# Attention loads on ScalarE's queue, a re-spaced order of attention groups and a wider spacing of Sinkhorn steps, ahead of a two-layer expert network

## The chip, the cores and the metric

One core of one Trainium2 chip. The metric is the device time of one execution in microseconds (us), lower is better. Engines: TensorE (PE; PEld is its weight load), VectorE (DVE), ScalarE (ACT), GpSimd (POOL) and SyncE (SP), which issues the DMAs.

## What is computed

Three stages, all in fp32. Attention over q, k, v of shape (4 batches, 8 heads, 576, 64), where the first four heads see a local band and the last four a stride:

```python
rel = pos[:, None] - pos[None, :]
mask_local = (rel >= 0) & (rel < 32)
mask_strided = (rel >= 0) & (pos[None, :] % 32 == pos[:, None] % 32)
attn = softmax(where(mask, q @ k.T / 8, -1e9));  x = attn @ v      # -> (2304, 512)
```

Then a mixture of eight experts with a dense gate, balanced by eight Sinkhorn steps:

```python
P = exp(x @ w_gate - max)
for _ in range(8):
    P /= P.sum(1, keepdims=True) + 1e-9
    P /= P.sum(0, keepdims=True) + 1e-9
    P *= N / E                                   # 2304 / 8
out = sum(P[:, e:e+1] * (relu(x @ w1[e]) @ w2[e]) for e in range(8))
```

and last a feed-forward layer, `h = out @ w_in; (h * sigmoid(1.702 * h)) @ w_out`, with 2048 hidden columns.

## The kernel before

The expert and feed-forward part is cut into units. A unit is one slice of 256 hidden columns for one block of 768 tokens; the first 32 units (4 per expert) belong to the first block. Each fp32 matrix is split into a high and a low part in fp32r, and each product is six matmuls. A unit of the first block is a list of 13 *pieces*: seven products that combine quarters of the input and of the weights (line 1038), and six pieces of the way back (`tile_down`, lines 1304 to 1306). Weights of the first block are loaded raw, split on ScalarE (high part, line 270 or 280) and GpSimd or DVE (low part, line 264), and stored split to DRAM from SyncE's queue (line 268) for the later blocks. `advance` issues the next piece and the side tasks that are due with it; side tasks are kept in a table by piece number. The program order of each engine's instructions is fixed by the order in which they are written; every engine works its own list in order, and so does SyncE with its DMAs.

Attention comes first and is software-pipelined over `groups` (line 876). A group (b, pair, g) with g of 0 to 2 is a third of the positions of one pair of local heads; (b, pair, -1), called compact, is a whole pair of strided heads, gathered by class. In step i, `att_step` writes scores for group i, the exponentials for group i - 1, normalisation for i - 2, the transpose for i - 3 and the products with v for i - 4, so 32 groups take 36 steps. A compact group's transpose (line 715, on DVE) is copied by four small copies into a block-diagonal operand, `wide` (lines 717 to 723), of which there is one. Its products with v (line 739) are evacuated on DVE (line 872). After the products of a compact group a filler comes before the next transpose, from step 10 on.

Between the parts of a step stand calls of a filler. In steps 0 to 9 it issues dummy matmuls (`keep_warm`, line 1451), IDLE_GAP of them per call; in steps 10 to 15 pieces at a rate of 0.6 per call and dummies otherwise; from step 16 on 1.5 pieces per call, three calls per step. Pieces 33, 35 and 37 hold no matmul.

The q/k tiles and the v tiles of attention have two buffers each (two early pairs have tiles of their own). `LOAD_QK` and `LOAD_V` give the step in which a pair's load is written: as early as the buffer's last reader is written, and not more than two steps ahead of the scores (three ahead of the products with v). The loads are issued by SyncE at the end of the step (lines 641, 648).

After the attention comes the gate: `gate_steps` is a list of small tasks, one for each piece from piece 106 on. A Sinkhorn iteration is `sinkhorn_rows` (five DVE operations, lines 985 to 992), three empty places, and `sinkhorn_cols` (one matmul, line 996, and four DVE operations, lines 998 to 1001), so five pieces. `last_rows` transposes the result on TensorE (line 1010). The experts' first twelve units don't use the gate yet.

Of the kernel before, what the change touches and what calls it, by code (L numbers as in the profile page):

```python
# [12 lines left out]
ALU = mybir.AluOpType  # L13
# [18 lines left out]
IDLE_FIRST = 6  # L32
IDLE_GAP = 1.0

# [23 lines left out]
def strided_attention_moe_ffn(  # L58
# [573 lines left out]

    def load_qk(b, pair, c=slice(0, S)):
        if (b, pair) in EARLY:
            if not spare:
                spare.append(tok.tile([P, 2, 2, S], F32, tag="tok", name="qkt"))
            t = spare[0][:, pair]
            nc.sync.dma_start(out=t[:, :, c], in_=qk[b, pair][:, :, c])
        else:
            t = ap.tile([P, 2, S], F32, tag="qk", name="qkt")  # L640
            nc.sync.dma_start(out=t, in_=qk[b, pair])
        att_in["qk", b, pair] = t

    def load_v(b, pair):
        t = ap.tile([P, CQ, P], F32, tag="v", name="vt")
        compact = pair >= NPAIR // 2
        src = vc[b, pair - NPAIR // 2] if compact else vw[b, pair]
        nc.sync.dma_start(out=t if compact else t[:, : vw.shape[3]], in_=src)
        att_in["v", b, pair] = t
# [62 lines left out]
    def compact_transpose(i, b, pair):  # L712
# [4 lines left out]
        for c in range(CG):  # L717
            rows = slice(c * Q, c * Q + CLEN)
            o = wide[rows, :, c * CLEN : (c + 1) * CLEN]
            if c % 2:  # L720
                nc.gpsimd.tensor_copy(o, src[rows, :, :CLEN])
            else:
                nc.scalar.activation(out=o, in_=src[rows, :, :CLEN], func=AF.Copy)
# [151 lines left out]

    groups = [(0, 0, 0), (0, 1, 0), (0, 0, 1), (0, 1, 1), (0, 2, -1), (0, 3, -1)]
    NHALF = len(groups)
    groups += [(0, 0, 2), (0, 1, 2), (1, 2, -1), (1, 3, -1), (1, 0, 0), (1, 1, 0)]
    NFIRST = len(groups)
    groups += [(1, 0, 1), (1, 0, 2), (1, 1, 1), (1, 1, 2)]  # L880
    for b in range(2, B):
        groups += [(b, pair, -1) for pair in PAIRS[:2]]
        groups += [(b, pair, g) for pair in PAIRS[2:] for g in range(3)]
    NALONE = NHALF + 1
# [8 lines left out]

    pairs = [(b, pair) for b in range(B) for pair in PAIRS]
    at = {p: [i for i, x in enumerate(groups) if x[:2] == p] for p in pairs}
# [10 lines left out]
    def att_step(i, fill):  # L906
# [3 lines left out]
        def run(d, stage):  # L910
# [5 lines left out]
            return stage(i - d, b, pair, g) or ()  # L916

        if i < NHALF + 4:
            for d, stage, gap in STAGES:
# [4 lines left out]
        else:  # L924
# [12 lines left out]
            for t in third[:1]:  # L937
                t()
            run(1, att_exp)
            fill()  # L940
            for t in third[1:]:
                t()
            fill()
        for p in LOAD_QK[i]:
            load_qk(*p)
        for p in LOAD_V[i]:
            load_v(*p)

# [45 lines left out]
    def sinkhorn_cols():  # L994
# [4 lines left out]
        nc.vector.reciprocal(out=cr, in_=cr)  # L999
        nc.vector.tensor_scalar_mul(cr, cr, float(NT) / E)  # L1000
        nc.vector.tensor_tensor(
            out=pr, in0=pr, in1=cr[:, None, :].to_broadcast([P, NTT, E]), op=ALU.mult
        )
# [11 lines left out]
    def gate_steps():  # L1015
        steps = [lambda blk=blk: gate_logits(blk) for blk in range(1, NB)] + [gate_max]
        steps += [lambda: None, gate_max_row, lambda: None, gate_max_all, lambda: None, gate_exp]
        for _ in range(SINKHORN):
            steps += [sinkhorn_rows, lambda: None, lambda: None, lambda: None, sinkhorn_cols]
        steps += [lambda: None, last_rows]  # L1020
        return steps
# [421 lines left out]
    with tc.manual_schedule():  # L1443
# [56 lines left out]

        ahead[NHALF + 1].append(lambda: split_input(0))
        ahead[NHALF + 3].append(lambda: split_input(3))
# [146 lines left out]
```

## Time and profile before

| | |
|---|---|
| median of 3 runs | 1975.1 us (1974.87 to 1975.49) |
| the profiled execution, its own time | 1973.61 us |
| its span, first to last instruction | 1971.8 us |
| PE busy, share of the span | 1920.8 us, 97% |
| DVE busy | 1456.3 us, 74% |
| POOL busy | 1248.0 us, 63% |
| ACT busy | 847.9 us, 43% |
| mean granted TensorE clock | 0.988 of 2.4 GHz |
| DMA | 546.19 MB, mean 277 GB/s |

Read it so: TensorE is the engine that is nearly always busy, and the chain of work that ended last runs through it for 74% of the span. What it lacks to full use lies early: the page's slices show it at 8 to 9 tenths in the first sixth of the span and at 9 or more from there on. Busy shares of a whole span hide this, so the rows below are taken by stage.

### The profile page before, as it was taken

How to read it: one execution, taken by the hardware profiler on the slowest of the kernel's cores; microseconds unless marked ns; L12 is line 12 of the kernel's file. 1: busy time of each engine (PE TensorE's matmuls, PEld its weight loads, DVE VectorE, ACT ScalarE, POOL GpSimd, SP SyncE). 2: the span in 40 equal slices, each digit the busy share in tenths (PEclk: the TensorE clock that was granted, in tenths of full speed). 3: DMA queues.
4: the chain of work that ended last, by engine and by line, in shares of the span. 5: the costliest groups of instructions: out<-in, count | busy, mean ns of one | idle time of the engine just before them, and what ended most of it. 6: DMA issues, size and time to landing. Idle time of an engine off the chain costs nothing.

```text
span 1971.8 us, 35140 instructions
## 1 busy us (share of the span) xinstructions
PE 1920.8 (97%) x11701; PEld 1794.1 (91%) x11701; DVE 1456.3 (74%) x2723; ACT 847.9 (43%) x2071; POOL 1248.0 (63%) x1290
## 2 busy tenths in 40 slices
PE   8988998999999999999999999999999999999999
PEld 6777787888888999999999999999999998888888
DVE  5776677676777788787877788888887766756555
ACT  4554455666766333333333433333333335533332
POOL 3555565786778677777677887888887767700100
PEclk7999999999999999999999999999999999999999
DMA  6557687999998888898998789999989867765653
GB/s 237 172 195 254 222 294 254 370 346 354 357 338 292 300 305 293 288 289 276 301 298 288 249 294 310 338 332 314 355 307 324 297 204 269 250 195 182 223 193 122
DMA packets 284452, 546.19 MB, mean 277 GB/s; under 512 B 30864, under 2 KB 52720, under 8 KB 283376
## 3 DMA queue, kind: packets, MB, share of 16 engines
q1 hardware_dynamic: 283984, 543.61, 80.4%
q8 instruction: 94, 1.54, 0.3%
q14 instruction: 86, 0.70, 0.1%
q10 hardware_dynamic: 288, 0.34, 0.1%
HBM read 382.30 MB, written 161.53 MB: 276 GB/s over the span
## 4 chain that ended last, share of the span: by engine, by line
PE 74%; DVE 3%; DMA 2%; POOL 1%; issue 1%; ACT 0%; SPq 0%; DVEq 0%; ACTq 0%; POOLq 0%
PE y L1199 22%; PE pA L1038 20%; PE pC L1038 10%; PE y L1306 6%; PE y L1305 6%; PE y L1304 5%; PE pB L1038 5%; DMA s1moe<-w 1%; DMA acc<-kept 0%; POOL s L1171 0%; DVE xs L565 0%; DMA w<-s7moe 0%; POOL comb L1146 0%; DMA s7moe<-w 0%; DVE r L1152 0%
## 5 line engine op out<-in xcount | busy, mean ns | idle before, releaser
L1038 PE MATMUL pA<-xc,w 128*128 128x384 f32 x2880 | 573.0, 336 | 2.2 <-DVE pB L1094 2.1
L1199 PE MATMUL y<-comb,w 128*128 128x384 f32 x2688 | 537.5, 334 | 2.5 <-DMA w<-s7moe 1.5
L1038 PEld LDWEIGHTS pA<-xc,w 128*128 128x128 f32 x2880 | 508.6, 188 | 19.4 <-DVE pB L1094 4.0
L1199 PEld LDWEIGHTS y<-comb,w 128*128 128x128 f32 x2688 | 472.1, 188 | 3.6 <-DVE r L1152 1.8
L1146 POOL TENSOR_TENSOR comb<-s,comb 128x384 fp32r<-128x384 f32 x256 | 283.5, 1118 | 87.2 <-ACT comb L1141 81.4
L1209 DVE TENSOR_TENSOR sum<-y,sum 128x384 f32<-128x384 f32 x420 | 231.0, 551 | 100.2 <-PE y L1199 98.0
L1038 PE MATMUL pC<-xc,w 128*128 128x384 f32 x1464 | 295.8, 336 | 0.0
L1306 PE MATMUL y<-w,hl 128*128 128x512 f32 x672 | 269.2, 401 | 5.8 <-DVE hl L1078 5.6
L1304 PE MATMUL y<-w,hh 128*128 128x512 f32 x672 | 265.4, 395 | 7.6 <-DVE x L863 3.5
L1038 PEld LDWEIGHTS pC<-xc,w 128*128 128x128 f32 x1464 | 259.7, 188 | 9.8
L1305 PE MATMUL y<-w,hh 128*128 128x512 f32 x672 | 267.0, 397 | 0.0
L1141 ACT ACTIVATE comb<-r 128x384 fp32r<-128x384 f32 x192 | 101.0, 526 | 365.8 <-DVE r L1152 354.8
L1306 PEld LDWEIGHTS y<-w,hl 128*128 128x128 f32 x672 | 126.9, 189 | 36.5 <-DVE hl L1078 9.0
L1304 PEld LDWEIGHTS y<-w,hh 128*128 128x128 f32 x672 | 127.1, 189 | 28.0 <-DVE x L863 4.1
L1038 PE MATMUL pB<-xc,w 128*128 128x384 f32 x708 | 142.1, 335 | 0.0
L270 ACT ACTIVATE w<-raw 128x256 fp32r<-128x256 f32 (+1 forms) x307 | 135.6, 460 | 14.2 <-POOL raw L234 11.5
L1305 PEld LDWEIGHTS y<-w,hh 128*128 128x128 f32 x672 | 127.0, 189 | 15.9
L1146 POOL TENSOR_TENSOR comb<-r,comb 128x384 fp32r<-128x384 f32 x64 | 67.6, 1056 | 116.2 <-ACT comb L1141 116.1
L264 POOL TENSOR_TENSOR w<-raw,w 128x512 fp32r<-128x512 f32 (+1 forms) x104 | 121.3, 1182 | 30.2 <-ACT w L270 30.0
L1141 ACT ACTIVATE comb<-s 128x384 fp32r<-128x384 f32 x256 | 131.5, 514 | 11.9 <-POOL s L1171 11.8
L1171 POOL TENSOR_TENSOR s<-r,r 128x384 f32<-128x384 f32 x127 | 135.1, 1084 | 2.1 <-DVE r L1152 2.0
L1333 DVE TENSOR_TENSOR acc<-y,acc 128x512 f32<-128x512 f32 x126 | 86.8, 689 | 63.7 <-PE y L1306 63.6
(179 smaller groups left out, 2824.0 us busy)
## 6 DMA issues: line engine op xcount, KB each, us to landing
w<-s1moe SPq DMA_DIRECT2D x448, 256.0 KB, 4.9
w<-s7moe SPq DMA_DIRECT2D x448, 256.0 KB, 4.9
s1moe<-w SPq DMA_DIRECT2D x216, 256.0 KB, 4.9
w<-s1ffn SPq DMA_DIRECT2D x133, 256.0 KB, 2.7
s7moe<-kw SPq DMA_DIRECT2D x116, 256.0 KB, 4.7
s7moe<-w SPq DMA_DIRECT2D x96, 256.0 KB, 4.8
w<-s2ffn SPq DMA_DIRECT2D x38, 512.0 KB, 3.7
raw<-wa SPq DMA_DIRECT2D x32, 512.0 KB, 6.0
```

The lines of the kernel that those rows point to most:

```text
L264: eng.tensor_tensor(out=t[:, 1], in0=src, in1=f(high), op=ALU.subtract)
L270: nc.scalar.activation(out=high, in_=src, func=AF.Copy)
L1038: nc.tensor.matmul(out=o, lhsT=w[:, hw, kk * P : (kk + 1) * P], rhs=x[:, hx, kk, :], start=opens and m == 0, stop=ends and m == len(todo) - 1,
L1141: nc.scalar.activation(out=t[:, 0, :], in_=part[i, q], func=AF.Copy)
L1146: eng.tensor_tensor(out=t[:, 1, :], in0=part[i, q], in1=f(t[:, 0, :]), op=ALU.subtract)
L1171: eng.tensor_tensor(out=part[i, q], in0=part[i, a], in1=part[i, b], op=op)
L1199: nc.tensor.matmul(out=o, lhsT=t[:, hw, dt * P : (dt + 1) * P], rhs=x[:, hx, :], start=(n == 0), stop=(n == 5))
L1209: nc.vector.tensor_tensor(out=a, in0=o, in1=a, op=ALU.add)
L1304: nc.tensor.matmul(out=o, lhsT=hh[:, c], rhs=w[:, 0], start=(m == 0), stop=False)
L1305: nc.tensor.matmul(out=o, lhsT=hh[:, c], rhs=w[:, 1], start=False, stop=False)
L1306: nc.tensor.matmul(out=o, lhsT=hl[:, c], rhs=w[:, 0], start=False, stop=(m == 1))
L1333: nc.vector.tensor_tensor(out=a, in0=y, in1=a, op=ALU.add)
```

## The change

- The q/k and v loads written by `LOAD_QK` and `LOAD_V` are issued from ScalarE's queue. From step 10 on they stand right after the exponentials of the step and not at its end.
- The groups of the first two batches are re-ordered so that no two compact groups are neighbours; for the last two batches the pairs come in the order 2, 0, 3, 1 (compact, three local thirds, compact, three local thirds).
- For the first twelve groups all four block-diagonal copies are made by ScalarE.
- IDLE_GAP is 1.5: 45 dummy matmuls in the first ten steps, which had 30.
- `split_input(0)` is written one step later (step 8).
- A Sinkhorn iteration takes six pieces, with four empty places, and `last_rows` has one more empty place ahead; the multiplication by N/E is merged with the one by the column factors.

```diff
-IDLE_GAP = 1.0
+IDLE_GAP = 1.5
...
-    def load_qk(b, pair, c=slice(0, S)):
+    def load_qk(b, pair, c=slice(0, S), q=nc.sync):
...
-            nc.sync.dma_start(out=t, in_=qk[b, pair])
+            q.dma_start(out=t, in_=qk[b, pair])
...
-    def load_v(b, pair):
+    def load_v(b, pair, q=nc.sync):
...
-        nc.sync.dma_start(out=t if compact else t[:, : vw.shape[3]], in_=src)
+        q.dma_start(out=t if compact else t[:, : vw.shape[3]], in_=src)
...
-            if c % 2:
+            if c % 2 and i >= NFIRST:
                 nc.gpsimd.tensor_copy(o, src[rows, :, :CLEN])
...
-    groups = [(0, 0, 0), (0, 1, 0), (0, 0, 1), (0, 1, 1), (0, 2, -1), (0, 3, -1)]
+    groups = [(0, 0, 0), (0, 1, 0), (0, 2, -1), (0, 0, 1), (0, 1, 1), (0, 3, -1)]
     NHALF = len(groups)
-    groups += [(0, 0, 2), (0, 1, 2), (1, 2, -1), (1, 3, -1), (1, 0, 0), (1, 1, 0)]
+    groups += [(0, 0, 2), (1, 2, -1), (0, 1, 2), (1, 3, -1), (1, 0, 0), (1, 1, 0)]
     NFIRST = len(groups)
     groups += [(1, 0, 1), (1, 0, 2), (1, 1, 1), (1, 1, 2)]
+    MIXED = (2, 0, 3, 1)
     for b in range(2, B):
-        groups += [(b, pair, -1) for pair in PAIRS[:2]]
-        groups += [(b, pair, g) for pair in PAIRS[2:] for g in range(3)]
+        for pair in MIXED:
+            groups += [(b, pair, g) for g in ((-1,) if pair >= NPAIR // 2 else range(3))]
...
-    pairs = [(b, pair) for b in range(B) for pair in PAIRS]
+    pairs = [(b, pair) for b in range(B) for pair in (PAIRS if b < 2 else MIXED)]
...
+        def loads():
+            for p in LOAD_QK[i]:
+                load_qk(*p, q=nc.scalar)
+            for p in LOAD_V[i]:
+                load_v(*p, q=nc.scalar)
...
             run(1, att_exp)
+            loads()
             fill()
...
-        for p in LOAD_QK[i]:
-            load_qk(*p)
-        for p in LOAD_V[i]:
-            load_v(*p)
+        if i < NHALF + 4:
+            loads()
...
-        nc.vector.tensor_scalar_mul(cr, cr, float(NT) / E)
-        nc.vector.tensor_tensor(
-            out=pr, in0=pr, in1=cr[:, None, :].to_broadcast([P, NTT, E]), op=ALU.mult
+        nc.vector.scalar_tensor_tensor(
+            out=pr,
+            in0=pr,
+            scalar=float(NT) / E,
+            in1=cr[:, None, :].to_broadcast([P, NTT, E]),
+            op0=ALU.mult,
+            op1=ALU.mult,
         )
...
-            steps += [sinkhorn_rows, lambda: None, lambda: None, lambda: None, sinkhorn_cols]
-        steps += [lambda: None, last_rows]
+            steps += [sinkhorn_rows] + [lambda: None] * 4 + [sinkhorn_cols]
+        steps += [lambda: None, lambda: None, last_rows]
...
-        ahead[NHALF + 1].append(lambda: split_input(0))
+        ahead[NHALF + 2].append(lambda: split_input(0))
```

## Rows read from the trace of the kernel before

**Rows 1.** Busy time by stage: length, PE, PEld, DVE, ACT, POOL, granted clock, DMA, GB/s.

```profile
0.00:47.50 47.50, 37.84 (x734) 28.20 (x735) 25.19 (x64) 20.09 (x70) 18.40 (x28) 0.71 0.67 231
47.50:80.50 33.00, 30.94 (x378) 25.38 (x376) 24.32 (x60) 18.91 (x68) 14.74 (x19) 1.00 0.46 161
80.50:262.00 181.50, 162.08 (x1468) 134.36 (x1468) 125.23 (x263) 86.19 (x266) 105.60 (x127) 0.96 0.65 230
262.00:325.30 63.30, 54.45 (x265) 47.35 (x264) 53.78 (x131) 32.26 (x89) 38.38 (x49) 0.97 0.80 281
387.00:449.50 62.50, 62.27 (x311) 55.59 (x310) 46.83 (x89) 41.79 (x117) 50.21 (x61) 1.00 0.98 345
700.00:1060.00 360.00, 360.00 (x2079) 360.00 (x2078) 291.31 (x540) 116.57 (x248) 256.62 (x251) 1.00 0.89 294
```

**Rows 2.** DMA issues in 4.5 to 5.5 us: count, KB each, median us to landing.

```profile
qkt<-qk SPq DMA_DIRECT2D x2, 576.0 KB, 7.8
```

**Rows 3.** SyncE's timeline: start, length, line, DMA.

```profile
4.61 1.46 SPq L641 DMA_DIRECT2D qkt<-qk  x2
...
174.81 0.59 SPq L648 DMA_DIRECT2D vt<-vc  x1
```

**Rows 4.** TensorE's timeline, opening: start, length, operation [idle before, releaser].

```profile
7.76 0.68 PE L770 MATMUL sc<-qkt 64*96 64x128 f32 x8
...
10.29 0.55 PE L827 MATMUL pt<-cst,e 96*128 96x96 f32 x4 [1.30 <-POOL e L816]
...
20.67 1.38 PE L665 MATMUL sc<-qkt 64*32 64x18 f32 x120 [3.01 <-issue]
...
27.38 0.69 PE L1451 MATMUL idle_out<-idle 128*128 128x384 f32 x1
...
28.84 1.01 PE L1451 MATMUL idle_out<-idle 128*128 128x384 f32 x2
...
39.17 1.93 PE L739 MATMUL av<-wide,vc 128*64 128x72 f32 x32 [2.62 <-POOL wide L721]
```

**Rows 5.** Busy time in 17.6 to 47.5 us, same columns as rows 1.

```profile
17.60:47.50 29.90, 23.11 (x523) 17.21 (x515) 15.98 (x40) 11.94 (x36) 13.55 (x19) 0.60 0.54 179
```

**Rows 6.** Groups by line and form, 0 to 360 us: busy, mean ns, idle before.

```profile
L723 ACT ACTIVATE wide<-eT 18x288 f32<-18x288 f32 x16 | 7.1, 443 | 24.9 <-DVE eT L715 24.7
...
L1000 DVE TENSOR_SCALAR sk<-sk 128x8 f32<-128x8 f32 x8 | 3.5, 436 | 0.3
```

**Rows 7.** TensorE's timeline, mixed steps.

```profile
119.03 0.52 PE L827 MATMUL pt<-cst,e 96*128 96x96 f32 x4 [2.71 <-DVE x L872]
...
166.69 1.22 PE L739 MATMUL av<-wide,vt 128*64 128x72 f32 x32
...
170.13 0.68 PE L770 MATMUL sc<-qkt 64*96 64x128 f32 x8
...
182.68 2.19 PE L739 MATMUL av<-wide,vt 128*64 128x72 f32 x32 [7.83 <-DMA vt<-vc]
184.80 1.98 PE L1038 MATMUL pA<-xc,w 128*128 128x384 f32 x6
```

**Rows 8.** SyncE's waits, 0 to 340 us: total, times, longest.

```profile
SPq L268 <- POOL w L264: 83.0, 26, 12.1
```

**Rows 9.** ScalarE's timeline, mixed steps.

```profile
175.36 0.40 ACT L802 ACTIVATE e<-e,st 96x128 f32<-96x128 f32 x1
...
183.91 0.42 ACT L270 ACTIVATE kw<-dsums 128x256 fp32r<-128x256 f32 x1 [5.61 <-DMA s7moe<-kw]
```

**Rows 10.** Sinkhorn's own instructions (tile sk): length, PE, PEld, DVE, ACT, clock, DMA.

```profile
263.25:324.98 61.73, 2.45 (x16) 2.81 (x16) 26.85 (x72) 0.00 (x0) 0.97 0.79 281
```

**Rows 11.** TensorE's timeline during Sinkhorn.

```profile
304.30 0.50 PE L1306 MATMUL y<-w,hl 128*128 128x512 f32 x1 [3.23 <-DVE hl L1078]
...
324.98 0.28 PE L1010 MATMUL ptr<-cst,pr 128*96 128x128 f32 x1 [3.65 <-DVE pr L1001]
```

## Prediction

> **What bounds the kernel now.** I read the busy time by stage first [rows 1]. From 700 us on TensorE is busy in every microsecond (360.00 of 360.00) at the full 2.4 GHz: there nothing but matmul work counts, and the change leaves that work as it is. So a gain or loss can arise only where TensorE still has gaps, in the first 325 us. The reader should subtract PE from the length in each earlier row: 9.7 us of gaps in 0 to 47.5, 2.1 in 47.5 to 80.5, 19.4 in 80.5 to 262, 8.9 in 262 to 325.3; 40 us in all. To these comes time at the lower clock: 0.71 of full in the first stage. TensorE's timeline then names the gaps, and the queues' views say why their releasers were late. Whatever is saved before 325 us should reach the end, since every later stage waits for TensorE itself.
>
> **The change, part by part.** Negative is a gain. The profiled execution took 1973.61 us for a span of 1971.8, and is 1.5 us below the median of the three timed runs, 1975.1; the sum is made against 1973.61 and 1.5 is added at the end.
>
> *First ten steps (0 to 47.5 us).* The first strided (compact) group moves from step 4 to step 2. Its scores need the third q/k load, which is issued at 4.61 us as the first of a pair that lands 7.8 us after issue in the median [rows 2, 3], so at about 12.4 us. TensorE reaches that step at 7.76 us [rows 4] and would stand until then. Before, the same stretch had 1.3 us of idling, a wait for the softmax of the first group [rows 4], which falls inside the new wait: net +3.3, between +2 and +4. IDLE_GAP 1.5 for 1.0 gives 45 dummy matmuls in thirty gaps for 30, 15 more. One further dummy in a gap costs 0.32 us at the lower clock (1.01 us for two, 0.69 for one [rows 4]) and half of that at full clock; three of them lie in the new wait, twelve cost 1.9 to 3.8, and I take 3.5, because the clock from 17.6 to 47.5 us is 0.60 [rows 5]. Against this, the two adjacent compact groups collided: the second one's transpose stood on DVE behind the first one's evacuation and behind the input split, so its block-diagonal copies came late and TensorE waited 2.62 us [rows 4]. With a local group between them and the split a step later that goes (-2.6). The 3.01 us "issue" wait in the second compact group's 128 small matmuls [rows 4] has no releaser that I can move on purpose; it may recur elsewhere, bounds -3 to 0, I take -1.5. Four block-diagonal copies in a row on ScalarE instead of two there and two on GpSimd make the operand ready two copies, 2 x 0.44 [rows 6] = 0.9 us, later; groups are now further apart, so 0 to +0.9 each for the four early groups, +0.6 in this stage in all. The input split now comes ahead of that group's evacuation, for which a local transpose waits: 0 to +2, I take +0.5. Sum so far +3.8. More dummies could also bring the clock back. At 0.60 the 23.1 us of PE in 17.6 to 47.5 [rows 5] contain at most 23.1 x 0.4 = 9 us of loss; I take a third of it, -3. **Stage: +1, between -7 and +8.**
>
> *Steps 10 to 15 (47.5 to 80.5 us).* 2.1 us of gaps [rows 1], one half of them around two adjacent compact groups. **-1, between -2 and +1.**
>
> *Mixed steps (80.5 to 262 us).* The largest single gap of the kernel is here: 7.83 us before the last compact group's products [rows 7]. Its cause is not the size of the load. The load stood in the program at the end of step 27, whose successor's products begin at 166.69 [rows 7]; SyncE issued it only at 174.81 [rows 3], 8.1 us later, because each store of split weights ahead of it waits for GpSimd's split (83 us in 26 waits, the longest 12.1 [rows 8]). On ScalarE's queue the load passes these stores, and in the new order the same load stands three steps ahead of its use, not two. After the gap TensorE was at the lower clock: the products took 2.19 us against 1.22, and the six matmuls after them 1.98 [rows 7], of which at most half is loss; I put 1.7 us on both. Together -9.5. *What is late next?* ScalarE. In the gap it sat until 183.91 us, 5.61 us, for the landing of a store whose tile it was to overwrite [rows 9]; with the load there in time, TensorE would soon want ScalarE's copy of a product. That store was issued right behind the two loads on the same queue; without them in front it should land earlier, but not all of this wait goes: +2.5, between 0 and +5.6. Loads on ScalarE also cost it their issue, 0.59 us on SyncE [rows 3]: 22 of them, 13 us of ScalarE, which is busy 86 of 181.5 us in 80.5 to 262 [rows 1]; I take +0.5, bounds 0 and +5. Behind an issue that waits are queued the ScalarE copies of products; 11 of the 22 loads overwrite a buffer whose last reader is in the same step. But the scores of step 28 ran at 170.13 and ScalarE's exponentials of that step, after which the load now stands, only at 175.36 [rows 7, 9]: the reader is done 5 us before, so I cost these waits at nothing; without that cover each would cost up to a microsecond.
>
> The 2.71 us wait of a transpose for DVE's evacuation of compact products [rows 7] came at an odd step, whose one filler piece holds no matmul. In the new order all compact groups of batches 2 and 3 have their products on even steps, with two filler pieces, all of them with matmuls. Between -2.7 and +1 (there are now four such places instead of two); I take -2.5. The remaining gaps of the stage I leave as they are. **Stage: -9, between -15 and -2.**
>
> The Trainium skill ("DMA: Bandwidth & Descriptors", Issuing engines are not separate DMA queues) speaks against this part: transfers started by different engines end up on the same 16 DMA engines, so another issuer saves only the time it takes to start them. By that alone the gap would stay. The trace shows a load held before issue, which is another thing than a slow transfer; the DMA share in that stage is 0.65 [rows 1].
>
> *Sinkhorn (262 to 325.3 us).* Eight iterations of five pieces, with what stands around them, lie between 263.25 and 324.98: 61.73 us for 41 pieces, 1.51 each. A unit of 13 pieces holds 42 + 36 = 78 matmuls; 387 to 449.5 holds 311 of them, four units [rows 1], so 15.6 us a unit and 1.20 a piece. With the small Sinkhorn matmuls that is 1.24. DVE is why: it is busy 53.78 of 63.3 us, 26.85 of them Sinkhorn [rows 1, 10], so 0.65 a piece of other work and 0.65 of Sinkhorn. After: one operation of 0.436 us [rows 6] leaves each iteration, 3.5 us in all (the fused multiplication may take 0.3 us less or more than the one it replaces), and 23.3 us of Sinkhorn spread over 50 pieces are 0.47 a piece; DVE needs 1.12. It reached 85% of the span before; at that share a piece takes 1.12 / 0.85 = 1.32. The same 50 pieces cost 41 x 1.51 + 9 x 1.20 = 72.7 before and 66 after: -6.7, and if no wait but the last one shrinks, -1. Waits that should shrink are 3.23 us for the low part of an activation, which stands on DVE behind a Sinkhorn step and 3.65 us for the final transpose [rows 11], which gets one more piece of cover. **-5, between -10 and 0.**
>
> **Sum.** +1 - 1 - 9 - 5 = -14: 1959.6 for the profiled execution, and with 1.5 for the median 1961.1.
>
> **The rivals.**
> (a) *Clock comes back in the first ten steps*, because more dummies and no collision leave no long hole: this stage gives -7 instead of +1, 1953. For it: the clock of 0.60 is that of the stretch that begins with the 3.01 us hole [rows 4, 5]. Against: the new hole at step 2 is longer. The Trainium skill ("TensorE: Matmul & The Clock Gate", What's actually happening) has the low clock as the default that activity releases, which would favour this case; [rows 5] show low clock beside 23.1 of 29.9 us of PE busy, so the trace agrees only in part.
> (b) *The gap turns into ScalarE's wait.* The load is there, but ScalarE still waits its 5.6 us for the store, and DVE, which no longer catches up in the gap, delays products; mixed steps give -3 and Sinkhorn -2: -5 in all, 1970. For it: [rows 9]. Against: DVE is busy only 69% of that stage [rows 1].
> (c) *The opening loses.* Low clock throughout, the 3 us hole recurs, the evacuation wait is new: +8 instead of +1, 1968.
> (d) *Slower: ScalarE is held by the loads.* 22 issues of 0.59 us and 11 waits of a microsecond are 24 us on an engine that TensorE's products wait for. If all of it lands on TensorE's path, 1961 + 24 = 1985; it decides from 14 us on, 0.64 us per load. Against: the 5 us between reader and issue.
>
> **How the numbers follow.** Forecast 1961 (own range 1953 to 1967) 0.46; (a) 0.13; (b) 0.22; (c) 0.10; (d) 0.09. What a measurement of this kernel can tell from no change is about 0.2%, 3.9 us, so faster means below 1971.2. Forecast, (a), (c) nearly whole and six tenths of (b) lie there: 0.80. Within 0.2%: the rest of (b), a part of (d) that is held only lightly: 0.11. Slower: 0.09. For the range I leave out (d) and the far ends of (a): 1948 to 1975.
>
> **What would show it.** The wait of products for the v load gone, and the loads' issue on ScalarE's queue within the step; PE idle in 80.5 to 262 down from 19 to some 11 us; a TensorE wait near 8 us for the third q/k load, four long; no 2.6 us wait for the block-diagonal operand; DVE's share in Sinkhorn at or under that of before over a stretch of 50 pieces, and the final transpose waiting under 2.5 us. I am wrong if ScalarE shows waits at the load lines, if its store waits are as long as the gap was, or if stage one ends after 52 us.

## The result, and the profile after

The changed kernel takes 1957.65 us (median of four runs, 1955.17 to 1963.4); the kernel before took 1975.3 us beside it. The ratio is 0.9912, 95% interval [0.9889, 0.9935]: 17.4 us less. The profiled execution took 1957.69 us with a span of 1955.9, so it stands for the median. The forecast was 1961, range 1948 to 1975. The sum came out; three of its four terms were wrong by more than the sum was (1.9 us on the profiled execution).

From gate logits 1 on only Sinkhorn and full TensorE are left, so I cut the span at three instructions that both programs have: the first product of the experts (step 10), the scores of step 16, and the first gate logits. The busy time between them, in the columns of rows 1, first of the kernel before and then of the changed one:

```profile
0.00:47.47 47.47, 37.81 (x733) 28.17 (x734) 25.16 (x64) 20.09 (x70) 18.40 (x28) 0.71 0.67 231
47.47:73.25 25.78, 23.72 (x221) 18.95 (x220) 19.64 (x49) 14.88 (x54) 11.75 (x15) 1.00 0.54 189
73.25:246.63 173.38, 153.96 (x1504) 128.77 (x1503) 120.91 (x252) 81.00 (x254) 97.95 (x117) 0.96 0.62 216
```

```profile
0.00:51.63 51.63, 37.66 (x744) 29.20 (x745) 28.16 (x68) 21.54 (x73) 17.70 (x25) 0.82 0.67 223
51.63:79.79 28.16, 26.41 (x224) 21.30 (x223) 18.88 (x45) 17.02 (x60) 9.52 (x11) 0.90 0.45 152
79.79:236.23 156.44, 149.47 (x1503) 124.79 (x1502) 122.62 (x252) 81.31 (x254) 98.85 (x117) 1.00 0.69 235
```

Read length minus PE in each row: that is TensorE's idle time. The forecast's stages ended at 80.5 and 262 us; the waits that it priced lie inside the stages cut here too.

| stage | before | after | difference | predicted |
|---|---|---|---|---|
| to the first product | 47.47 | 51.63 | +4.2 | +1 |
| to the scores of step 16 | 25.78 | 28.16 | +2.4 | -1 |
| to gate logits 1 | 173.38 | 156.44 | -16.9 | -9 |
| from there to the end | 1725.2 | 1719.7 | -5.5 | -5 |
| span | 1971.8 | 1955.9 | -15.9 | -14 |

The opening's loss is all idle time (9.66 us before, 13.97 after; PE busy is 0.15 us less). Each stage is read from one execution: two executions of one and the same program (the first experiment and its repetition) took 46.16 and 48.05 us to the first product. Over all runs below it comes at 45.8 to 49.8 us with the old order of the first groups and at 48.8 to 52.0 with the new one. The 2.4 us behind it aren't idle (2.06 before, 1.75 after): the granted clock was 0.90, not 1.00. The mixed stage gained 12.45 us of idle time (19.42 to 6.97) and 4.49 us of busy time (the clock went from 0.96 to 1.00).

TensorE's timeline of the changed kernel, the waits that answer to rows 4, 7 and 11 (start, length, operation, in brackets the idle time before it and its releaser):

```profile
12.56 1.40 PE L665 MATMUL sc<-qkt 64*32 64x18 f32 x128 [3.89 <-DMA qkt<-qk]
...
24.21 1.22 PE L739 MATMUL av<-wide,vc 128*64 128x72 f32 x32 [1.29 <-ACT wide L723]
...
27.09 0.87 PE L827 MATMUL pt<-cst,e 96*128 96x96 f32 x4 [1.29 <-DVE x L872]
...
40.45 2.19 PE L739 MATMUL av<-wide,vc 128*64 128x72 f32 x32 [3.29 <-ACT wide L723]
...
45.36 0.52 PE L827 MATMUL pt<-cst,e 96*128 96x96 f32 x4 [1.78 <-DVE x L872]
...
171.22 0.55 PE L827 MATMUL pt<-cst,e 96*128 96x96 f32 x4 [0.82 <-DVE x L872]
...
197.88 1.22 PE L739 MATMUL av<-wide,vt 128*64 128x72 f32 x32
...
320.14 0.27 PE L1020 MATMUL ptr<-cst,pr 128*96 128x128 f32 x1
```

The last compact group's products (197.88) wait for nothing, where before they waited 7.83 us for their v load [rows 7]; the final transpose waits for nothing, where it waited 3.65 us [rows 11]. Five waits of 1.3 to 3.9 us stand in the opening. The third q/k load is one that was predicted, to the size. The wait for the block-diagonal operand, which the change was to take away (2.62 us in [rows 4]), is still there at 40.45, and longer.

### The profile page after: what moved, and what is told of

It is laid out like the page before. It is cut to its first block, busy times and chain, and to the rows that moved or that the text cites. A ratio compares the mean times of both kernels' runs of the same rounds, so it can differ in the third digit from the quotient of the medians.

```text
span 1955.9 us, 35146 instructions
## 1 busy us (share of the span) xinstructions
PE 1917.5 (98%) x11716; PEld 1792.3 (92%) x11716; DVE 1455.9 (74%) x2715; ACT 853.1 (44%) x2079; POOL 1244.9 (64%) x1282
## 4 chain that ended last, share of the span: by engine, by line
PE 62%; DVE 2%; DMA 2%; POOL 2%; issue 1%; ACT 0%; SPq 0%; ACTq 0%; DVEq 0%; POOLq 0%
PE y L1209 21%; PE pA L1048 17%; PE pC L1048 9%; PE pB L1048 4%; PE y L1316 4%; PE y L1315 4%; PE y L1314 4%; DMA w<-s1moe 1%; POOL s L1181 1%; DMA w<-s7moe 1%; POOL comb L1156 1%; DMA rows<-prd 0%; DVE xs L565 0%; DMA ws<-fw 0%; DVE r L1162 0%
```

## Experiments

Six parts are told apart by letters. **L**: the loads on ScalarE's queue in the middle of the step. **M**: the pair order 2, 0, 3, 1 of the last two batches. **S**: the Sinkhorn spacing with the merged multiplication. **O**: the order of the first twelve groups with `split_input(0)` a step later. **C**: four block-diagonal copies on ScalarE. **G**: IDLE_GAP 1.5. The full change is all six. My theory: L takes the gap by passing SyncE's waiting stores, M spreads the compact groups, S relieves DVE, and O, C and G together give nothing or a loss. Rivals: the gain comes from one part alone; the place of the load in the step matters and not its queue; the opening's loss is one wait.

Each time is a median of four to six runs, each ratio against runs of the kernel before on the same chip; a gain in us that stands behind a ratio is worked out from it. What one profiled execution shows of a stage is given by the time from gate logits 0 to the gate's maximum (*mixed*) and from there to the end (*tail*): 162.8 and 1717.0 us before, 146.7 and 1711.2 after.

### Three parts, the opening as before (LMS)

Against the changed kernel:

```diff
-IDLE_GAP = 1.5
+IDLE_GAP = 1.0
...
-            if c % 2 and i >= NFIRST:
+            if c % 2:
...
-    groups = [(0, 0, 0), (0, 1, 0), (0, 2, -1), (0, 0, 1), (0, 1, 1), (0, 3, -1)]
+    groups = [(0, 0, 0), (0, 1, 0), (0, 0, 1), (0, 1, 1), (0, 2, -1), (0, 3, -1)]
...
-    groups += [(0, 0, 2), (1, 2, -1), (0, 1, 2), (1, 3, -1), (1, 0, 0), (1, 1, 0)]
+    groups += [(0, 0, 2), (0, 1, 2), (1, 2, -1), (1, 3, -1), (1, 0, 0), (1, 1, 0)]
...
-        ahead[NHALF + 2].append(lambda: split_input(0))
+        ahead[NHALF + 1].append(lambda: split_input(0))
```

> All of the change except its first twelve groups: order, split of the input, block-diagonal copies and IDLE_GAP are those of before; loads on ScalarE's queue, the mixed order of batches 2 and 3 and the Sinkhorn spacing are those of after. Theory: TensorE reached the scores of step 16 at 79.8 us after the change against 73.3 before, so the new opening costs 6.5 us that nothing later gives back: this kernel should be that much faster than the changed one, 1951. Rival: the later opening lets GpSimd and ScalarE get ahead, so that the mixed steps run without holes only because of it; then the old opening brings back some 6 us of gaps there and the time is 1957 to 1959.

Measured: 1954.06 us, ratio 0.9890 [0.9876, 0.9905], mixed 149.5, tail 1711.1. The three parts carry more than the whole gain; undoing the other three is worth some 4 us, less than the 6.5 expected: 2.8 us of what the old opening saves go back in the mixed steps (149.5 for 146.7), as the rival had it.

### The loads alone (L)

Against the kernel before:

```diff
...
+        def loads():
+            for p in LOAD_QK[i]:
+                load_qk(*p, q=nc.scalar)
+            for p in LOAD_V[i]:
+                load_v(*p, q=nc.scalar)
...
             run(1, att_exp)
+            loads()
             fill()
...
-        for p in LOAD_QK[i]:
-            load_qk(*p)
-        for p in LOAD_V[i]:
-            load_v(*p)
+        if i < NHALF + 4:
+            loads()
```

> The kernel before with the loads on ScalarE's queue after the exponentials, nothing else. Theory (the gap is SyncE's lateness): the 7.8 us wait for the last compact v load shrinks to under 3 us and the time falls by 5 to 8 us, to 1968 to 1970. Rival (the order of groups makes the difference, the loads would come in time anyway with three steps of lead): ScalarE is itself about 5 us behind at that place, the load is issued hardly earlier, and the time is within 3 us of before.

Measured: 1970.61 us, ratio 0.9968 [0.9955, 0.9981], so -6.3 us; mixed 157.0, tail 1717.2. ScalarE's queue issued the last v load at 168.07 (SyncE had at 174.81 [rows 3]): 73.1 and 82.8 us after gate logits 0. TensorE's waits around that place:

```profile
177.58 1.22 PE L739 MATMUL av<-wide,vt 128*64 128x72 f32 x32 [0.58 <-issue]
182.07 0.55 PE L827 MATMUL pt<-cst,e 96*128 96x96 f32 x4 [2.02 <-DVE x L872]
```

The 7.83 us are gone, and the next in line is late by 2.02 us: the transpose behind the compact group's evacuation on DVE. The gain of 6.3 us is about what is left of the gap after that. Queue and place were changed together here, so this run doesn't tell which of them did it.

### The mixed order alone (M)

```diff
+    MIXED = (2, 0, 3, 1)
     for b in range(2, B):
-        groups += [(b, pair, -1) for pair in PAIRS[:2]]
-        groups += [(b, pair, g) for pair in PAIRS[2:] for g in range(3)]
+        for pair in MIXED:
+            groups += [(b, pair, g) for g in ((-1,) if pair >= NPAIR // 2 else range(3))]
...
-    pairs = [(b, pair) for b in range(B) for pair in PAIRS]
+    pairs = [(b, pair) for b in range(B) for pair in (PAIRS if b < 2 else MIXED)]
```

> The kernel before with the mixed order of batches 2 and 3 alone; loads stay on SyncE. Theory: SyncE is still held by stores of split weights, so a wait of 3 us or more for a v or q/k load remains and the time falls by 3 to 6 us, to 1969 to 1972, from the 2.7 us wait for the evacuation and the clock. Rival (order): the load's lead of three steps is enough without the other queue, the gap is gone, and the time falls by 10 us or more, to 1965 or less.

Measured: 1967.66 us, ratio 0.9955 [0.9940, 0.9971], so -8.9 us; mixed 153.85, tail 1717.1. That is more than the 3 to 6 us expected and less than the rival's 10. The order alone may give more than the loads alone, but the two intervals overlap, and the profiled execution was the fastest of this kernel (1963.23). In the mixed steps TensorE's wait for DVE's evacuation fell from 2.7 to 0.7 us. A v load is late here too, another one. SyncE's timeline and TensorE's:

```profile
167.89 1.06 SPq L648 DMA_DIRECT2D vt<-vw  x1
```

```profile
174.79 0.91 PE L851 MATMUL av<-eT,vt 128*64 128x96 f32 x8 [5.34 <-DMA vt<-vw]
```

### The Sinkhorn part alone (S)

```diff
-        nc.vector.tensor_scalar_mul(cr, cr, float(NT) / E)
-        nc.vector.tensor_tensor(
-            out=pr, in0=pr, in1=cr[:, None, :].to_broadcast([P, NTT, E]), op=ALU.mult
+        nc.vector.scalar_tensor_tensor(
...
-            steps += [sinkhorn_rows, lambda: None, lambda: None, lambda: None, sinkhorn_cols]
-        steps += [lambda: None, last_rows]
+            steps += [sinkhorn_rows] + [lambda: None] * 4 + [sinkhorn_cols]
+        steps += [lambda: None, lambda: None, last_rows]
```

> The kernel before with six pieces for a Sinkhorn iteration and the merged multiplication, nothing else. Theory: -5 us, 1970, from the wait for the final transpose (3.65 us) and the one behind an iteration (3.2 us). Rival: the waits move to other instructions behind the same clumps on DVE, and the time is within 2 us of before.

Measured: 1969.53 us, ratio 0.9965 [0.9953, 0.9978], so -6.9 us; tail 1710.3 (-6.7), mixed 165.9 (+3.1, in one execution). The part doesn't touch that stage: from gate logits 0 to 1 TensorE was busy 137.87 us for 135.45 with the same 1150 matmuls, at a granted clock of 0.94 for 0.96, so most of it is the clock.

The three parts add, within the error: -6.3 - 8.9 - 6.9 = -22.1 us, each known to 2.5 or 3 us, and together they gave -21.7.

### The first compact group one step later

Against the changed kernel:

```diff
-    groups = [(0, 0, 0), (0, 1, 0), (0, 2, -1), (0, 0, 1), (0, 1, 1), (0, 3, -1)]
+    groups = [(0, 0, 0), (0, 1, 0), (0, 0, 1), (0, 2, -1), (0, 1, 1), (0, 3, -1)]
```

> The changed kernel with the first compact group in step 3 and not in step 2 (it changes places with a local group). Theory: the 3.9 us for which TensorE stood before the scores of step 2 was the landing of the third q/k load, so one step later this wait falls to under 2 us; the time falls by 2 to 3 us against the changed kernel, to 1955. Rival: the hole only moves to the operand or evacuation waits that follow (1.3, 1.3, 3.3 and 1.8 us in the changed kernel), and the time stays at 1957 to 1958.

Measured: 1957.26 us, ratio 0.9910 [0.9895, 0.9925]. TensorE's waits in the opening:

```profile
12.75 1.31 PE L665 MATMUL sc<-qkt 64*32 64x18 f32 x128 [1.31 <-DMA qkt<-qk]
...
38.80 2.19 PE L739 MATMUL av<-wide,vc 128*64 128x72 f32 x32 [3.89 <-ACT wide L723]
...
43.68 0.87 PE L827 MATMUL pt<-cst,e 96*128 96x96 f32 x4 [1.76 <-DVE x L872]
```

The wait for the q/k load went from 3.89 to 1.31 us and the first product came at 48.83 instead of 51.63; other waits stayed (3.89 us for the operand, 1.76 for the evacuation). The median is 0.4 us lower, as the rival had it, but each interval reaches 3 us or more to either side. In the profiled execution 1.4 of the 2.8 us are left at the end: 0.9 were lost up to gate logits 0 and 1.8 in the mixed steps, and the tail was 1.2 shorter. What this one wait is worth at the end stays open.

### The dummy matmuls (LMS and G)

Against LMS:

```diff
-IDLE_GAP = 1.0
+IDLE_GAP = 1.5
```

> Loads on ScalarE, mixed order and Sinkhorn spacing with the opening of before (the first experiment of this study, 1954.1), and IDLE_GAP 1.5 added. Theory: 15 more dummy matmuls cost their 0.16 to 0.32 us each and do not hold the clock: 2.5 to 5 us more, 1957 to 1959. Rival: they hold the clock at 2.4 GHz in the first 47 us, where it was 0.71 of full; the time falls by 3 us or more, to 1951.

Measured: 1953.5 us, ratio 0.9892 [0.9877, 0.9906]; first product at 47.05 (LMS: 46.16 and 48.05). Neither the loss of 2.5 to 5 us nor the gain of 3 came. Against the two measurements of LMS (1954.06 and 1950.56) fifteen more dummies cost between nothing and some 3 us.

### The order of the first groups (LMS and O)

Against LMS:

```diff
-    groups = [(0, 0, 0), (0, 1, 0), (0, 0, 1), (0, 1, 1), (0, 2, -1), (0, 3, -1)]
+    groups = [(0, 0, 0), (0, 1, 0), (0, 2, -1), (0, 0, 1), (0, 1, 1), (0, 3, -1)]
...
-    groups += [(0, 0, 2), (0, 1, 2), (1, 2, -1), (1, 3, -1), (1, 0, 0), (1, 1, 0)]
+    groups += [(0, 0, 2), (1, 2, -1), (0, 1, 2), (1, 3, -1), (1, 0, 0), (1, 1, 0)]
...
-        ahead[NHALF + 1].append(lambda: split_input(0))
+        ahead[NHALF + 2].append(lambda: split_input(0))
```

> As the first experiment (1954.1), with the new order of the first twelve groups and the later input split added, but two of the four block-diagonal copies on GpSimd and IDLE_GAP 1.0. Theory: the order carries the wait for the third q/k load (3.9 us, of which 1.3 were there before) and the waits for DVE's evacuation after the split, and gives back the 3.6 us operand wait: +1 to +3, 1955 to 1957. Rival: the order is worth its place and copies and dummies are what cost: -2, 1952.

Measured: 1955.73 us, ratio 0.9903 [0.9888, 0.9918]. Its first product comes at 51.96, as in the full change, so O has the opening's loss by itself, but in another form:

```profile
0.00:51.96 51.96, 41.97 (x729) 31.43 (x730) 27.35 (x64) 19.56 (x68) 18.72 (x28) 0.90 0.64 214
```

```profile
20.46 1.17 PE L770 MATMUL sc<-qkt 64*96 64x128 f32 x8
...
41.90 2.19 PE L739 MATMUL av<-wide,vc 128*64 128x72 f32 x32 [2.21 <-POOL wide L721]
...
46.51 0.90 PE L827 MATMUL pt<-cst,e 96*128 96x96 f32 x4 [1.80 <-DVE x L872]
```

TensorE was idle for 9.99 us, as before (9.66), and busy for 41.97 instead of 37.81. The column's 0.90 hides why: this execution's trace has no record of the clock before 38 us, and the column counts such time as full speed. The scores at 16.26, 20.46 and 31.05 us took 1.17 us each, which is their time at the low level (0.68 at the high one [rows 4]). So O alone ran most of its opening at the low clock with little idling, and the full change at a higher clock with 4 us more of idling; both reach the first product at 51.6 to 52.0. That the new order costs as much when the clock is up can't be read from this execution. Part of the loss comes back: mixed is 147.1 with O and 149.5 without.

### The spacing without the merge (LM and half of S)

Against LM:

```diff
-            steps += [sinkhorn_rows, lambda: None, lambda: None, lambda: None, sinkhorn_cols]
-        steps += [lambda: None, last_rows]
+            steps += [sinkhorn_rows] + [lambda: None] * 4 + [sinkhorn_cols]
+        steps += [lambda: None, lambda: None, last_rows]
```

> Loads on ScalarE, mixed order, opening of before, six pieces for a Sinkhorn iteration, but the multiplication by N/E still an instruction of its own. Theory (DVE's work per piece decides): the spacing gives four fifths of the Sinkhorn gain and the merged instruction, 0.44 us eight times, the rest: 1 us slower than the first experiment, 1955. Rival: only the chain of one iteration counts, and the separate instruction adds 0.44 x 8 = 3.5 us to it: 1957.5 or more.

Measured: 1957.48 us, ratio 0.9911 [0.9895, 0.9928], tail 1714.6. That is the rival's number (1957.5), but the stretch doesn't show the rival's reason. From the gate's maximum to the final transpose, in the columns of rows 1, the kernel before, this one and the changed one:

```profile
254.77:324.98 70.21, 61.36 (x297) 52.99 (x297) 58.30 (x142) 36.97 (x102) 44.50 (x57) 0.98 0.78 277
```

```profile
244.34:319.42 75.08, 71.67 (x352) 62.84 (x351) 61.31 (x152) 40.99 (x112) 50.04 (x62) 0.98 0.84 290
```

```profile
244.72:320.14 75.42, 71.66 (x350) 63.01 (x351) 59.81 (x148) 42.35 (x115) 52.95 (x66) 0.98 0.86 300
```

TensorE's idle time is 8.85, 3.41 and 3.76 us: the spacing alone takes away all that the two parts take away. In the executions with both parts this stretch lasts 72.1 to 75.4 us, so 75.1 without the merge isn't out of their range. The tail of the spacing alone is 2.6 to 5.3 us longer than those of the executions with both (1709.3 to 1711.9), and its time is 3.4 and 6.9 us above the two measurements of LMS, where only the interval of the first overlaps with its own. So the merge may be worth some us at the end, but not by what DVE does in the Sinkhorn stretch, and where they come from stays open.

What the instructions cost DVE: shortest, median and longest of eight (ns), of the kernel before, of the spacing alone and of the changed kernel:

```profile
L1000 DVE TENSOR_SCALAR sk<-sk x8: 171/390/880, 269.4 to 323.4; 128x8 f32<-128x8 f32 x8
L1001 DVE TENSOR_TENSOR pr<-pr,sk x8: 307/800/1360, 269.6 to 324.1; 128x144 f32<-128x144 f32 x8
```

```profile
L1007 DVE TENSOR_TENSOR pr<-pr,sk x8: 309/553/1351, 261.3 to 317.7; 128x144 f32<-128x144 f32 x8
```

```profile
L1006 DVE SCALAR_TENSOR_TENSOR pr<-pr,sk x8: 307/385/1045, 260.9 to 317.1; 128x144 f32<-128x144 f32 x8
```

At its shortest the fused instruction takes what the multiplication takes, 0.31 us, and the one that goes took 0.17. All that is above lies beside work of GpSimd, as the last section shows, so the means of two kernels can't be compared as prices of the instructions.

### The input split later, in the old order (LMS, G and the split)

Against LMS and G:

```diff
-        ahead[NHALF + 1].append(lambda: split_input(0))
+        ahead[NHALF + 2].append(lambda: split_input(0))
```

> Loads on ScalarE, mixed order, Sinkhorn spacing, IDLE_GAP 1.5 and the old order of the first groups (the sixth experiment, 1953.5), with the input split one step later. Theory: the 4.3 us that TensorE waited there for the block-diagonal operand at 39 us are DVE's: the second compact group's transpose stands behind the input split, which waits for ScalarE; a step later this falls to under 2 us, and the time falls by 1.5 to 3 us, to 1951. Rival: the split then stands ahead of the evacuation of that group's products, a transpose waits for it instead (1.8 us in the changed kernel), and the time stays within 1 us of 1953.5.

Measured: 1953.85 us, ratio 0.9895 [0.9882, 0.9909]. The wait for the block-diagonal operand fell from 4.32 us (LMS and G, at 39.32) to 2.45 (at 37.72), and behind it the transpose waits 1.30 us for the evacuation; the end is the same as with the split a step earlier (1953.5), as the rival had it. One wait takes the place of the other.

### The loads on SyncE's queue, in the middle of the step (LMS and G)

Against LMS and G:

```diff
             for p in LOAD_QK[i]:
-                load_qk(*p, q=nc.scalar)
+                load_qk(*p, q=nc.sync)
             for p in LOAD_V[i]:
-                load_v(*p, q=nc.scalar)
+                load_v(*p, q=nc.sync)
```

> The sixth experiment (1953.5) with the loads written at the same place in the step, after the exponentials, but issued by SyncE. Theory: the queue matters, not the place; SyncE is late behind the stores of split weights, TensorE waits 4 us or more for a v load at 165 to 185 us, and the time is 4 to 7 us longer, 1957.5 to 1960. Rival: the place in the step and the mixed order give SyncE enough lead; within 1.5 us of 1953.5.

Measured: 1952.52 us, ratio 0.9889 [0.9876, 0.9903], mixed 148.8; LMS and G on ScalarE's queue gave 1953.5 and 149.1. The same load as in M alone, on SyncE's timeline:

```profile
162.64 0.60 SPq L641 DMA_DIRECT2D qkt<-qk  x1
163.29 0.61 SPq L648 DMA_DIRECT2D vt<-vw  x1
```

TensorE's only waits from 160 to 200 us:

```profile
168.40 0.55 PE L827 MATMUL pt<-cst,e 96*128 96x96 f32 x4 [0.72 <-DVE x L872]
...
198.44 0.50 PE L1314 MATMUL y<-w,hh 128*128 128x512 f32 x1 [0.94 <-DVE acc L1329]
```

No product waits for a v load in this kernel, against the theory. So with the mixed order the queue is not what matters. What M alone lacked was the place: half a step earlier in the program the same queue issued the load at 163.29 instead of 167.89 (69.1 and 77.4 us after gate logits 0). SyncE's timelines show what it passes: in M one raw load, which waits there until 162.37 us, and seven stores are issued from 159.28 us on ahead of the two attention loads; here the same eight follow the attention loads, the raw load at 167.10. M differs from this kernel in S and G too, which lie outside this stage.

### The first one again (LMS)

The same program as the first experiment.

> The kernel of the first experiment unchanged. Its profile showed the clock at 0.76 from 58 to 72 us, that of the sixth 1.00 behind the same two waits, 0.97 and 0.95 us, for the operand and the evacuation. Theory: whether the clock falls there is not fixed by the program; in another execution of the same kernel it stays at 1.00, piece 20 is reached 3 us earlier, and the runs scatter by 3 to 5 us. Rival: the program fixes it (the loads on ScalarE, or fewer dummies, bring it): 0.76 again and the same times within 0.5 us in this profile's first 95 us.

Measured: 1950.56 us, ratio 0.9880 [0.9867, 0.9894], the fastest median of all. Its interval overlaps with that of the first one (1954.06). Two measurements of one program differ by 3.5 us in the median, and the last section tells where the two traces part. A difference of this size between two of these kernels is therefore not settled by one run of each.

### The copies on ScalarE (LMS and C)

Against LMS:

```diff
-            if c % 2:
+            if c % 2 and i >= NFIRST:
```

> The first experiment (1954.1) with the four block-diagonal copies of the first twelve groups on ScalarE, nothing else added. Theory: the operand is ready 0.9 us later where TensorE already waits for it (3.6 us at 39 us, 1.0 us at 58 us): +1 to +2, 1955 to 1956. Rival: GpSimd, relieved of 0.86 us a group, delivers splits earlier and the two cancel: within 1 us of 1954.1.

Measured: 1955.95 us, ratio 0.9912 [0.9896, 0.9927]; the profiled execution was its slowest, 1962.54. TensorE's timeline, last compact group of the first two batches:

```profile
63.06 1.24 PE L739 MATMUL av<-wide,vc 128*64 128x72 f32 x32 [2.05 <-ACT wide L723]
```

The same products waited 0.97 and 0.95 us, for GpSimd's copies, in the two executions of LMS. So four copies in a row make this operand about 1.1 us later at this place. The ratio lies 0.002 to 0.003 above the two of LMS, with an interval that overlaps with that of the first and just misses that of the second: C costs 0 to some 6 us, more likely a loss than nothing.

## Why the prediction was right, and where not

**The sum** was right because two errors cancelled, which is luck: one mechanism was worth more than forecast, the other less. By the ratios L, M and S together are worth 22 to 24 us, and O, C and G take 4 to 6 back; each of these is known to some 3 us. I had 14 for the first three and about nothing for the others.

**The opening (+1 predicted; +4.2 and another +2.4 measured).** The step that failed is that the gains of this stage were real. The q/k wait was sized rightly: 3.89 us for "about four". But the collision of two compact groups, which I let go for -2.6, didn't go: the operand comes at 40.45, after a wait of 3.29 us. ScalarE's timeline shows why:

```profile
38.55 0.45 ACT L723 ACTIVATE wide<-eT 18x288 f32<-18x288 f32 x1 [2.86 <-DVE eT L715]
38.73 0.33 ACTq L641 DMA_DIRECT2D qkt<-qk  x1
39.02 1.38 ACT L723 ACTIVATE wide<-eT 18x288 f32<-18x288 f32 x3
```

DVE's transpose of that group begins at 37.82, behind other DVE work that leaves no gap from 34.55 us on, and four copies of 0.45 us follow in a row. Then the evacuation, which I had priced at 0.5 because the input split now comes ahead of it, made TensorE wait 1.78 us. DVE's timeline:

```profile
36.22 1.23 DVE L814 TENSOR_SCALAR st<-st 96x4 f32<-96x4 f32 x1
...
42.46 1.57 DVE L581 TENSOR_TENSOR xc<-x,xc 128x768 fp32r<-128x768 f32 x1 [2.44 <-ACT xc L576]
43.96 0.44 DVE L705 TENSOR_REDUCE stc<-e 128x16 f32<-128x288 f32 x1
...
44.81 0.75 DVE L872 COPY x<-av 128x288 f32<-128x288 f32 x2
```

The first of these lines is ahead of the transpose: an operation that takes 0.15 to 0.17 us elsewhere in this opening takes 1.23 us beside a GpSimd split that ends at 37.42, so by my estimate the transpose came 1.1 us later for it. The split waits 2.44 us for ScalarE's part, which stands behind the four copies on that engine (at 41.60), and holds the evacuation behind it. It would do so without C: in the run of O alone, where GpSimd makes two of the copies, the operand's wait is 2.21 us and the evacuation's 1.80. So C lengthens the first wait by 1.1 us, and the second comes with the later split; it stood in the old order too when only the split was moved (1.30 us).

The other terms: the 3.01 us "issue" hole of [rows 4], of which I kept half, didn't recur in this execution, so that term was undersized in the other direction. The dummies, at +3.5, cost between nothing and some 3 us at the end. The third of the clock's 9 us that I counted on (-3) brought nothing: granted clock 0.82 for 0.71 and PE busy 37.66 for 37.81, because the time is spent on dummies and idle. Of rival (c)'s three conditions one came, the evacuation's wait, with +4.2 in the stage and not +8; the stage ended 0.4 us short of the 52 us that I had named as a sign of being wrong. Rival (a) fails in its last step: the clock did come back, but the first product came only 0.3 us earlier than in the run of O alone at the low clock.

**Steps 10 to 15 (-1 predicted, +2.4).** Not idle time (1.75 us for 2.06) but the low clock, 0.90; the last section shows that such a stretch comes and goes in one and the same program. Whether any of it belongs to the change stays open.

**The mixed steps (-9 predicted, -16.9).** The gap went as predicted. Three terms were mis-sized. ScalarE's store wait, for which I put +2.5, doesn't reach TensorE, which waits for ScalarE 0.7 us in all there, after 0.8 before. ScalarE's waits in 79.8 to 252.2 us (total, times, longest), the two for a store's landing:

```profile
ACT dsums L270 <- DMA s7moe<-dsums: 6.2, 3, 3.1
...
ACT kw L270 <- DMA s7moe<-kw: 1.4, 2, 1.1
```

The longest for kw is 1.1 us where it was 5.61 [rows 9]; those for dsums are 6.2 us in three where they were 4.3 in two. So rival (b) falls, though the waits for stores aren't gone. The clock was put at -1.7, for the matmuls right behind the gap; over the stage it was worth 4.49 us of PE busy time at equal work (1504 and 1503 matmuls). And the further gaps, left "as they are", shrank: idle time fell by 12.45, of which the gap (7.83) and the transposes' wait (2.71, put at -2.5; at most 0.82 now) make no more than 10.54.

The reason was wrong in one point, and no stage's time would have shown it. I had put the gap down to SyncE's queue. With the order of M the loads on SyncE's queue are in time too, if they stand in the middle of the step (1952.5 against 1953.5 us). The place in the program, and the one more step of distance, cured it. The Trainium skill ("DMA: Bandwidth & Descriptors", Issuing engines are not separate DMA queues), which had been weighed against this part, says that another issuing engine saves only the time of starting the transfer. With the place the same, these two runs agree. What isn't settled: SyncE in mid-step with the old order, and ScalarE's queue at the end of the step, weren't tried; so for L alone the queue may still be what counts.

**Rival (d), ScalarE held by the loads.** An issue takes 0.33 us on ScalarE's queue in the median and 0.39 at most (38.73 above), against 0.59 on SyncE [rows 3], and lies beside its own activations: it begins at 38.73, while the copy of 38.55 to 39.00 runs, and ends beside the next ones. No wait at lines 641 or 648 stands among ScalarE's waits in 79.8 to 252.2 us. Of the 22 loads, which I had set against this stage, 14 lie in it. The predicted +0.5 was nearer to nothing.

**Sinkhorn (-5 predicted, -5.5).** Right in sum, but not in how the two parts share it. From the gate's maximum to the final transpose there are nine more pieces, and the stretch grew from 70.2 to 75.4 us; nine pieces at the 1.20 us of full TensorE would be 10.8, so 5.6 were gained, of which 3.65 is the final transpose's wait. The spacing alone needs 75.1, so it gains 5.9 by the same reckoning: the merge, which took 3.5 us from DVE in my sum, adds nothing in this stretch. The sum held DVE's share at 85% and let its work set the pace; by the rows of the spacing experiment that share is 83% before, 82% with the spacing and 79% with both, and TensorE's idle time doesn't follow it. I had costed the fused multiplication like the one it replaces, and at 0.31 us for either that was right. The DVE time of tile sk in 250 to 320 us, of the kernel before, of spacing alone and of the changed kernel:

```profile
250.00:320.00 70.00, 3.20 (x20) 3.19 (x20) 25.80 (x71) 0.40 (x1) 0.98 0.79 278
```

```profile
250.00:320.00 70.00, 2.36 (x16) 2.87 (x16) 25.20 (x72) 0.40 (x1) 0.98 0.84 290
```

```profile
250.00:320.00 70.00, 2.51 (x16) 3.16 (x16) 20.76 (x64) 0.40 (x1) 0.98 0.84 293
```

The spacing leaves DVE's Sinkhorn work nearly where it was, and the merge takes 4.4 to 5 us of it, without a gain of TensorE that shows here.

**A better kernel.** L, M and S with the opening of before (1950.6 and 1954.1), with G (1953.5), or with G and SyncE as the issuer (1952.5) all have lower medians than the full change (1957.65), as has the input split a step later (1953.85). Each interval overlaps with that of the full change, [0.9889, 0.9935], so none is settled by itself; that five medians out of five lie 3.6 to 7.1 us below speaks for leaving O and C out.

## What to carry to other kernels

When a load is late, look first at where it stands in its queue's program and only then at which queue it is: with the mixed order, half a step earlier was worth as much as another engine's queue. Spacing colliding groups apart paid in the mixed steps, where two pieces of products fill the place between them, and not in the opening, where the engine that they collide on, DVE, has no gap; that reason is read from the traces and was not tried by itself. Work taken off an engine that is busy beside the bottleneck is not yet time gained: the merge took 4.4 to 5 us off DVE, and TensorE's idle time in that stretch stayed as it was.

## What the runs showed of the hardware

The granted clock fell or stayed behind nearly the same waits, in the same program. The first and the second LMS execution, 58 to 72 us, in the columns of rows 1:

```profile
58.00:72.00 14.00, 13.05 (x105) 10.04 (x101) 6.76 (x18) 7.48 (x30) 5.22 (x5) 0.76 0.43 147
```

```profile
58.00:72.00 14.00, 12.10 (x115) 9.42 (x114) 9.54 (x24) 9.82 (x38) 6.08 (x7) 1.00 0.43 147
```

TensorE's timeline of the first, then of the second:

```profile
57.78 1.22 PE L739 MATMUL av<-wide,vc 128*64 128x72 f32 x32 [0.97 <-POOL wide L721]
...
60.32 0.87 PE L827 MATMUL pt<-cst,e 96*128 96x96 f32 x4 [0.95 <-DVE x L872]
61.12 1.17 PE L770 MATMUL sc<-qkt 64*96 64x128 f32 x8
```

```profile
59.30 1.22 PE L739 MATMUL av<-wide,vc 128*64 128x72 f32 x32 [0.95 <-POOL wide L721]
...
61.84 0.52 PE L827 MATMUL pt<-cst,e 96*128 96x96 f32 x4 [0.95 <-DVE x L872]
62.30 0.68 PE L770 MATMUL sc<-qkt 64*96 64x128 f32 x8
```

Waits of 0.97 and 0.95 us stand ahead of the transpose in the one, 0.95 and 0.95 in the other; then the scores take 1.17 us at the low level or 0.68 at the high one. From the first product to gate logits 0 the first execution needs 47.96 us and the second 44.64. That is 3.3 us, of which the first had a lead of 1.9; at the end of the span it is 3.9 behind, and 1.8 of that arise after the gate's maximum. The executions of the kernel before, of M, S and four others had 1.00 in this stretch, those of L, of the spacing and of C 0.76, the changed kernel and its variant with the compact group in step 3 0.88. A forecast of this kernel can't tell on which side a run falls, and a difference of 3 us between two of them says little until this stretch has been looked at.

One and the same DVE instruction has very different lengths. The multiplications of tile pr by factors of tile sk (128x144) took 307 to 310 ns in every instance that had no GpSimd instruction beside it, in the kernel before, the spacing alone and the changed kernel, fused or not; every instance above 330 ns had one beside it. The longest, 1360 ns at 313.73 us of the kernel before, ran beside GpSimd's splits of a weight (312.38 to 314.93). So a mean over such instructions also tells what GpSimd was doing at the time.
